# Placing the last attention pieces of a batch ahead of one or two layer-2 pieces, and copying the last two output halves with VectorE alone

## The chip, the cores and the metric

The kernel runs on one core of a Trainium2 chip. The metric is device time in microseconds (us), the median of several executions. Before the change it is 332.97 us (three runs, 332.66 to 333.33). The profiled execution has a span of 331.5 us; all times inside it are counted from its start. The granted TensorE clock was 0.998 of full speed.

## The reference

Eight batches of 576 tokens with eight heads of 64 go through causal attention in which heads 0 to 3 see only the last 32 positions (local) and heads 4 to 7 only positions with the same remainder by 32 (strided). The attention output, 4608 tokens of 512, then goes through two layers with a leaky activation between them:

```python
scores = scale * q @ k.T                      # per batch and head, scale = 1/8
attn = softmax(where(mask, scores, -1e9))     # mask: local or strided, causal
x = (attn @ v)            # -> tokens x (heads * 64) = 4608 x 512
h = x @ w_in              # 4608 x 2048
g = maximum(h, 0) + alpha * minimum(h, 0)
out = g @ w_out           # 4608 x 512, float32
```

## The kernel before, in words

**Two streams of work on one TensorE.** The layers work on nine chunks n = 0 to 8 of 512 tokens. For each chunk there are 16 pieces of layer 1 (`lin1_piece`, L534) and then 16 of layer 2 (`lin2_piece`, L563). The attention of the eight batches is cut into small pieces, held in one fixed list (`pieces`, L389 to L514). The pieces of the list are dealt out between the pieces of the layers, always in the same order; the program order of every engine is the order of this Python code, since each instruction is wrapped in `keep`.

**A layer-1 piece** multiplies a 512-token stretch of xT by one 128-column slice of w_in: four matmuls kk = 0 to 3 (L544) into a PSUM tile "hps". Slice kk of xT holds the two heads of pair kk of a batch, so the fourth matmul needs pair 3. ScalarE writes the negative part (L554), VectorE combines it into gT (L557). This last operation, `fin`, is emitted after the attention piece that follows the layer piece (list `late`, L522 to L529). **A layer-2 piece** is a quarter, called part, of an output tile mt = 0 to 3 of 128 tokens: four matmuls (L586) into "ops". With part 3 ScalarE copies the tile to SBUF (L591) and the SyncE queue sends it to memory (L592). Both layers share one pool of three PSUM buffers, tag "hps".

**The attention pieces** of a pair g of heads (four pairs a batch, the first two local, the last two strided; b = g // 4):

- T: transposes of q or k on TensorE (`transpose_piece`, L221), copies to qT by VectorE and to kT by ScalarE.
- S g.0 and S g.1 (`score_piece`, L275): score matmuls (L295), exponential by ScalarE (L319), mask by GpSimd (L329).
- P g.0 to P g.2 (`pv_piece`, L331): matmuls with v (L345), then a reciprocal (L352) and a multiplication (L354) by VectorE.
- X g (`x_piece`, L359): transposes of the result on TensorE (L362), and a copy into xT by ScalarE for strided pairs (L366), by VectorE for local ones (L370).

From batch 2 on, pairs 0 to 2 of a batch have no X piece. Their result goes through a DMA transpose on the SyncE queue (`x_dma`, L372): directly into xT for the local pairs (L378), and for pair 2 into a tile xs (L376), which ScalarE copies into xT (`x_copy`, L381 to L385). `x_copy` of pair g - 2 is emitted with piece S g.1 (L512), so for pair 10 with S12.1. Also from batch 2 on, q and k of the strided pairs are loaded with a cast by the GpSimd queue (`load_d`, L118) and turned by two DMA transposes on the SyncE queue (`transpose_d`, L124, L128). For batch 3 these are emitted with the last P piece of pair 11 (L506), and the first to read them is S14.0.

**How the pieces are dealt out.** In chunk 0 the batch-1 pieces are dealt out by an explicit rule (L700 to L704): after layer-2 piece i that many pieces of the list, and what is left after the last piece. From chunk 1 on a counter does it (L709 to L725). `left` is the number of pieces that must be out by the end of the chunk so that the next batch is complete; the counter grows by half a share with each layer-1 piece and by a whole share with each layer-2 piece:

```python
acc += left / (23.5 - 0.5 * skip) * (0.5 if i < 16 else 1.0)
cnt = int(acc); acc -= cnt
attn_n(cnt, ab)                     # cnt pieces of the list follow here
```

`left` is 27 in chunk 1 (with skip = 4: the first four layer-1 pieces get none), 21 in chunks 2 to 5, 15 in chunk 6, and zero in chunks 7 and 8. The last piece of each of these stretches is the X piece of the batch's last pair (X11, X15 ... X31). With the divisor 23.5 it comes out behind the last layer-2 piece of the chunk.

**The end.** The last output tile (chunk 8, mt = 3) is computed in two halves of 256 columns (L570 to L584). Each half is copied by ScalarE (128 columns, L581) and VectorE (128 columns, L582) into one tile "osb" and sent by one DMA (L583).

Of the kernel before, what the change touches and what calls it, by code (L numbers as in the profile page):

```python
# [31 lines left out]
def kernel(  # L32
# [10 lines left out]
    nc = tc.nc  # L43
    keep = tc.keep_in_program_order
# [401 lines left out]
    end1 = len(pieces)  # L446


    for g in range(7, npair + 2):
# [33 lines left out]
        for i, (kind, fn) in enumerate(seq):  # L483
            extra = []
            if todo and i in nslots:
                left = len([z for z in nslots if z >= i])
# [31 lines left out]
    def attn_until(b):  # L518

        return max(i for i, (g, _) in enumerate(pieces) if g == 4 * b + 3) + 1  # L520
# [3 lines left out]
    def attn_step(end):  # L524
        if pos["i"] < end:
            pieces[pos["i"]][1]()
            pos["i"] += 1
        while late:
            late.pop(0)()  # L529
# [4 lines left out]
    def lin1_piece(n, m):  # L534
        if m == 0:
            gTs[n] = gpool.tile([128, 16, 512], F16, tag="gT", name="gT")
        c0 = (512 * n) % RING
        parts = [(c0, 0, min(512, RING - c0))]
        if c0 + 512 > RING:
            parts.append((0, RING - c0, 512 - (RING - c0)))  # L540
        hps = phpool.tile([128, 512], F32, tag="hps", name="hps")
        for kk in range(4):
            for x, (src, dst, w) in enumerate(parts):
                keep(nc.tensor.matmul(  # L544
                    hps[:, dst : dst + w],
                    win16[:, kk, 128 * m : 128 * m + 128],
                    xT[:, kk, src : src + w],
                    start=(kk == 0 and x == 0),
                    stop=(kk == 3 and x == len(parts) - 1),
                    skip_group_check=True,  # L550
                ))

        neg = npool.tile([128, 512], F32, tag="neg", name="neg")
        keep(nc.scalar.activation(neg, hps, AF.Relu, scale=-1.0))  # L554

        def fin():
            keep(nc.vector.scalar_tensor_tensor(  # L557
                gTs[n][:, m, :], neg, oma[:, m : m + 1], hps, op0=ALU.mult, op1=ALU.add))
        late.append(fin)
# [3 lines left out]
    def lin2_piece(n, i):  # L563
        mt, part = i // 4, i % 4
        last = n == NCH - 1
        if part == 0:
            ops_cur["t"] = phpool.tile([128, 512], F32, tag="hps", name="ops")
        ops = ops_cur["t"]
        r0 = 512 * n + 128 * mt
        if last and mt == 3:  # L570

            if part in (1, 3):
                return
            c0 = 128 * part
            half = phpool.tile([128, 512], F32, tag="hps", name="ops3") if part else ops
            for kf in range(16):
                keep(nc.tensor.matmul(  # L577
                    half[:, 0:256], gTs[n][:, kf, 128 * mt : 128 * mt + 128],
                    wout16[:, kf, c0 : c0 + 256], start=(kf == 0), stop=(kf == 15)))
            osb = opool.tile([128, 512], F32, tag="osb", name="osb")  # L580
            keep(nc.scalar.copy(osb[:, 0:128], half[:, 0:128]))  # L581
            keep(nc.vector.tensor_copy(osb[:, 128:256], half[:, 128:256]))  # L582
            keep(nc.sync.dma_start(out[r0 : r0 + 128, c0 : c0 + 256], osb[:, 0:256]))  # L583
            return  # L584
        for kf in range(4 * part, 4 * part + 4):
            keep(nc.tensor.matmul(  # L586
                ops, gTs[n][:, kf, 128 * mt : 128 * mt + 128], wout16[:, kf, :],
                start=(kf == 0), stop=(kf == 15)))
        if part == 3:
            osb = opool.tile([128, 512], F32, tag="osb", name="osb")  # L590
            keep(nc.scalar.copy(osb, ops))  # L591
            keep(nc.sync.dma_start(out[r0 : r0 + 128, :], osb))  # L592
# [84 lines left out]
    def attn_n(n, end):  # L677
        for _ in range(n):
            attn_step(end)
        if n == 0:  # L680
            attn_step(0)
# [17 lines left out]
        attn_n(0, end1)  # L699
    for i in range(16):  # L700
        lin2_piece(0, i)
        attn_n(0 if i < 1 else 2 if i < 10 else 1, end1)
    while pos["i"] < end1:
        attn_step(end1)  # L704
    wide["on"] = False
# [3 lines left out]
    for n in range(1, NCH):  # L709
        ab = attn_until(n + 1) if n + 1 < B else len(pieces)  # L710
        left = ab - pos["i"]
        skip = 4 if n == 1 else 0
        acc = 0.0
        for i in range(32):
            if i < 16:
                lin1_piece(n, i)
            else:
                lin2_piece(n, i - 16)
            if i >= skip:
                acc += left / (23.5 - 0.5 * skip) * (0.5 if i < 16 else 1.0)  # L720
            cnt = int(acc)
            acc -= cnt
            attn_n(cnt, ab)
        while pos["i"] < ab:
            attn_step(ab)  # L725
# [30 lines left out]
```

The softmax here doesn't subtract the row's maximum and nothing guards it: scores larger than these inputs give would overflow.

## Time and profile before

| What | Value |
|---|---|
| median time, span of the profile | 332.97 us, 331.5 us |
| TensorE busy, share of the span | 319.1 us, 96% |
| VectorE, ScalarE, GpSimd busy | 183.0, 171.8, 141.2 us |
| chain that ended last, by engine | PE 89%, ACT 4%, DVE 3%, DMA 2% |
| layer-1 matmuls (L544), layer-2 matmuls (L586) | 640 and 560 |
| output DMA of a full tile, issue to landing, median | 2.3 us |
| xs transpose, issue to landing, median | 2.7 us |

PE is TensorE's matmul row and PEld its weight loads, which overlap with it. DVE is VectorE, ACT ScalarE, POOL GpSimd, SP the SyncE queue, which only issues DMAs and waits. L544 is line 544 of the kernel, and "hps<-xT,win" is what the instruction writes and reads. A row of the timeline has the start, the duration, the engine and line, the operation and its shape, and how often it is merged ("x3"); in brackets stands the idle time of the engine before it and what ended that idle time. The chain of waits is followed back from the last instruction, so its rows are what the end of the kernel hung on. The ends of matmuls are modelled in the profile, their starts are recorded.

### The profile page before, as it was taken

How to read it: one execution, taken by the hardware profiler on the slowest of the kernel's cores; microseconds unless marked ns; L12 is line 12 of the kernel's file. 1: busy time of each engine (PE TensorE's matmuls, PEld its weight loads, DVE VectorE, ACT ScalarE, POOL GpSimd, SP SyncE). 2: the span in 40 equal slices, each digit the busy share in tenths (PEclk: the TensorE clock that was granted, in tenths of full speed). 3: DMA queues.
4: the chain of work that ended last, by engine and by line, in shares of the span. 5: the costliest groups of instructions: out<-in, count | busy, mean ns of one | idle time of the engine just before them, and what ended most of it. 6: DMA issues, size and time to landing. Idle time of an engine off the chain costs nothing.

```text
span 331.5 us, 6272 instructions
## 1 busy us (share of the span) xinstructions
PE 319.1 (96%) x2493; PEld 161.6 (49%) x2493; DVE 183.0 (55%) x358; ACT 171.8 (52%) x297; POOL 141.2 (43%) x152
## 2 busy tenths in 40 slices
PE   7899999999998999999999999999999999999995
PEld 2554455554553445444458654445444444444444
DVE  5477836477544873387428832783368238605800
ACT  2644753458456645575457544764477237415611
POOL 7932495117986366736583628332611400000000
PEclk9999999999999999999999999999999999999999
DMA  7999999699599459774978397517730130011011
GB/s 221 194 205 206 248 207 154 109 211 210 105 159 179 163 69 162 122 203 55 172 114 216 37 153 125 106 17 106 139 57 18 51 96 21 1 74 52 2 63 63
DMA packets 77596, 40.32 MB, mean 122 GB/s; under 512 B 58480, under 2 KB 69248, under 8 KB 77568
## 3 DMA queue, kind: packets, MB, share of 16 engines
q0 software_dynamic: 41728, 17.38, 49.6%
q1 hardware_dynamic: 35840, 22.55, 29.9%
q8 instruction: 19, 0.31, 0.4%
q14 instruction: 9, 0.07, 0.1%
HBM read 38.01 MB, written 9.44 MB: 143 GB/s over the span
## 4 chain that ended last, share of the span: by engine, by line
PE 89%; ACT 4%; DVE 3%; DMA 2%; issue 1%; SPq 0%; ACTq 0%
PE hps L544 37%; PE ops L586 37%; PE sp L295 4%; PE pv L345 4%; PE tp L235 2%; DMA kl<-in_k_dram 2%; DVE x L354 1%; PE wps L608 1%; PE ops L577 1%; ACT xT L366 1%; ACT osb L591 1%; PE sph L311 1%; PE sp L311 1%; ACT kT L175 1%; DVE qT L177 1%
## 5 line engine op out<-in xcount | busy, mean ns | idle before, releaser
L544 PE MATMUL hps<-xT,win 128*128 128x512 f16 (+1 forms) x640 | 134.1, 358 | 3.4 <-ACT xT L366 2.8
L586 PE MATMUL ops<-wout,gT 128*128 128x512 f16 x560 | 137.0, 379 | 0.0
L557 DVE SCALAR_TENSOR_TENSOR gT<-neg,oma,hps 128x512 f16<-128x512 f32 x144 | 105.9, 744 | 51.3 <-ACT neg L554 43.6
L554 ACT ACTIVATE neg<-hps 128x512 f32<-128x512 f32 x144 | 86.0, 597 | 46.3 <-PE hps L544 45.2
L329 POOL TENSOR_TENSOR et<-et,consts 128x576 f16<-128x576 f16 (+1 forms) x48 | 61.1, 1275 | 94.3 <-ACT et L319 94.2
L544 PEld LDWEIGHTS <-win 128*128 128x128 f16 x640 | 59.6, 98 | 60.8 <-issue 7.3
L586 PEld LDWEIGHTS <-gT 128*128 128x128 f16 x560 | 48.3, 98 | 45.9
L319 ACT ACTIVATE et<-sp 72x576 f16<-72x576 f32 (+1 forms) x56 | 36.2, 646 | 30.9 <-PE sp L295 17.0
L591 ACT COPY osb<-ops 128x512 f32<-128x512 f32 x35 | 20.5, 586 | 49.9 <-PE ops L586 46.0
L352 DVE RECIPROCAL rc<-pv 72x6 f32<-72x6 f32 (+2 forms) x80 | 14.9, 186 | 55.0 <-PE pv L345 54.9
L354 DVE TENSOR_TENSOR x<-pv,rc 96x384 f16<-96x384 f32 (+2 forms) x62 | 33.0, 532 | 2.1
L345 PEld LDWEIGHTS <-et 72*128 72x128 f16 (+1 forms) x448 | 23.6, 98 | 16.8 <-DVE x L354 1.1
L295 PEld LDWEIGHTS <-kT 64*128 64x128 f16 x448 | 10.8, 95 | 26.2 <-issue 21.2
L295 PE MATMUL sp<-qT,kT 64*128 64x72 f16 (+1 forms) x392 | 17.0, 201 | 1.9 <-ACT kT L175 1.9
L608 PE MATMUL wps<-wrm 128*128 128x512 f16 x44 | 16.2, 442 | 1.2 <-DVE wrm L620 1.2
L177 DVE COPY qT<-tp 128x1024 f16<-128x1024 f16 (+1 forms) x10 | 10.1, 1010 | 11.7 <-PE tp L235 11.7
L167 POOL DMA_DIRECT2D vl<-in_v_dram x8 | 11.2, 1396 | 11.8 <-PE xp L362 10.5
L345 PE MATMUL pv<-vs,et 72*128 72x65 f16 x256 | 15.2, 194 | 0.1
L179 POOL COPY vs<-stv 72x1024 f16<-72x1024 f16 x14 | 14.4, 1034 | 0.0
L175 ACT COPY kT<-tp 128x1024 f16<-128x1024 f16 (+1 forms) x10 | 8.4, 843 | 7.4 <-PE tp L235 7.4
L383 ACT COPY xT<-xs 128x576 f16<-128x576 f16 x6 | 7.8, 1302 | 7.6 <-DMA xs<-x16s 7.6
L345 PE MATMUL pv<-vl,et 128*128 128x65 f16 x192 | 11.1, 194 | 0.0
(73 smaller groups left out, 162.9 us busy)
## 6 DMA issues: line engine op xcount, KB each, us to landing
out_dram<-osb SPq DMA_DIRECT2D x35, 256.0 KB, 2.3
ql<-in_q_dram SPq DMA_DIRECT2D x6, 512.0 KB, 5.9
kl<-in_k_dram SPq DMA_DIRECT2D x6, 512.0 KB, 6.3
stv<-in_v_dram POOLq DMA_DIRECT2D x8, 288.0 KB, 7.1
vl<-in_v_dram POOLq DMA_DIRECT2D x6, 384.0 KB, 10.6
win<-in_moe_w_in_dram POOLq DMA_DIRECT2D x4, 512.0 KB, 9.5
wout<-in_moe_w_out_dram POOLq DMA_DIRECT2D x4, 512.0 KB, 17.1
qsd<-in_q_dram POOLq DMA_DIRECT2D x6, 288.0 KB, 6.2
```

Of the source, the lines that this page charges most:

```text
L295: keep(nc.tensor.matmul(sps[y][:, w * x : w * x + w], P.kT[hf, k0 : k0 + 128], P.qT[hf, q0 : q0 + w], start=(x == 0), stop=(x == len(grp) ...
L319: keep(nc.scalar.activation(ev.rearrange("r (y c) -> r y c", y=2), sp[0:r, :, 0:n], AF.Exp, scale=SCALE))
L329: keep(nc.gpsimd.tensor_tensor(ev, ev, m, op=ALU.mult))
L345: keep(nc.tensor.matmul(pv[:, 65 * x : 65 * x + 65], et[0:r, c : c + 128], v16[0:r, 2 * P.pr + hh, t, :] if P.strided else v16[:, 6 * (2 * ...
L352: keep(nc.vector.reciprocal(rc[0:w, 0:nb], pvv[:, :, 64]))
L354: keep(nc.vector.tensor_tensor(P.x16[0:w, c0 : c0 + 64 * nb].rearrange("r (c e) -> r c e", e=64), pvv[:, :, 0:64], rc[0:w, 0:nb].unsqueeze ...
L544: keep(nc.tensor.matmul(hps[:, dst : dst + w], win16[:, kk, 128 * m : 128 * m + 128], xT[:, kk, src : src + w], start=(kk == 0 and x == 0) ...
L554: keep(nc.scalar.activation(neg, hps, AF.Relu, scale=-1.0))
L557: keep(nc.vector.scalar_tensor_tensor(gTs[n][:, m, :], neg, oma[:, m : m + 1], hps, op0=ALU.mult, op1=ALU.add))
L586: keep(nc.tensor.matmul(ops, gTs[n][:, kf, 128 * mt : 128 * mt + 128], wout16[:, kf, :], start=(kf == 0), stop=(kf == 15)))
L591: keep(nc.scalar.copy(osb, ops))
L608: keep(nc.tensor.matmul(wps, wrm[:, 0:128], wrm, start=True, stop=True))
```

## The change

Three edits. In chunk 0, two attention pieces instead of one follow layer-2 pieces 10 to 12, so that the list's stretch is through before the last layer-2 piece. From chunk 1 on the divisor is 22.5 instead of 23.5, so that the counter runs a little faster and one or two layer-2 pieces follow the last attention piece of a batch. This is meant to let the work on that last piece end under layer-2 matmuls instead of in front of the next chunk's layer 1. And the last two output halves are each copied by one VectorE copy of 256 columns, instead of 128 by ScalarE and 128 by VectorE.

```diff
@@ lin2_piece, the last output tile
             osb = opool.tile([128, 512], F32, tag="osb", name="osb")
-            keep(nc.scalar.copy(osb[:, 0:128], half[:, 0:128]))
-            keep(nc.vector.tensor_copy(osb[:, 128:256], half[:, 128:256]))
+            keep(nc.vector.tensor_copy(osb[:, 0:256], half[:, 0:256]))
             keep(nc.sync.dma_start(out[r0 : r0 + 128, c0 : c0 + 256], osb[:, 0:256]))
@@ chunk 0
     for i in range(16):
         lin2_piece(0, i)
-        attn_n(0 if i < 1 else 2 if i < 10 else 1, end1)
+        attn_n(0 if i < 1 else 2 if i < 13 else 1, end1)
@@ chunks 1 to 8
             if i >= skip:
-                acc += left / (23.5 - 0.5 * skip) * (0.5 if i < 16 else 1.0)
+                acc += left / (22.5 - 0.5 * skip) * (0.5 if i < 16 else 1.0)
```

The pieces around the places that matter, before and after (l1 m and l2 i are the pieces of layer 1 and 2, and what is named follows behind them):

| Stretch | Before | After |
|---|---|---|
| chunk 0 | l2 10 X6, l2 11 X7, l2 12 P4.0, l2 13 P4.1, l2 14 P5.0, l2 15 P5.1 X4 X5 | l2 10 X6 X7, l2 11 P4.0 P4.1, l2 12 P5.0 P5.1, l2 13 X4, l2 14 X5, l2 15 nothing |
| chunk 1 | l2 9 P10.2 S12.0, l2 10 P11.0, l2 11 S12.1 (with x_copy of pair 10), l2 12 P11.1, l2 13 P11.2 S13.0, l2 14 P12.0, l2 15 X11 | l2 8 P10.2, l2 9 S12.0 P11.0, l2 10 S12.1 (with x_copy), l2 11 P11.1, l2 12 P11.2 S13.0, l2 13 P12.0, l2 14 X11, l2 15 nothing |
| chunks 2 to 5, layer 1 (chunk 2 named) | l1 8 P13.0, l1 11 S14.1, l1 13 P13.1, l1 15 S15.0 | l1 8 P13.0, l1 10 S14.1, l1 12 P13.1, l1 14 S15.0 |
| chunks 2 to 6, end (chunk 2 named) | l2 14 P16.0, l2 15 X15 | l2 13 P16.0, l2 14 X15, l2 15 nothing |

In chunk 2, S14.0 stands behind layer-1 piece 6 before and after.

## The prediction

> **What bounds the kernel now.** I read the page first, then the chain of waits in order of time, the list of who waited for whom, and the timeline at the places where the chain leaves TensorE.
>
> ```profile
> PE 319.1 (96%) x2493; PEld 161.6 (49%) x2493; DVE 183.0 (55%) x358; ACT 171.8 (52%) x297; POOL 141.2 (43%) x152
> ```
>
> TensorE is busy 96% of the span and every other engine about half, so time can only come out of stretches in which a matmul starts later than it could. The yardstick is in the chain:
>
> ```profile
> 66.59 5.12 PE hps L544 x23
> ...
> 286.22 13.81 PE ops L586 x64
> ```
>
> 64 matmuls of 512 columns in 13.81 us are 0.216 us each, so a layer piece of four takes 0.863 us. All delays below are start to start against 0.216, since the idle time that the page gives hangs on modelled ends of matmuls. The longest repeated TensorE wait in the list of waits is the one the change aims at:
>
> ```profile
> PE hps L544 <- ACT xT L366: 2.8, 6, 1.2
> ```
>
> Six waits, one at each boundary between chunks 1 to 6 and the next. The boundary after chunk 2 in the timeline:
>
> ```profile
> 137.45 0.59 ACT L591 COPY osb<-ops 128x512 f32<-128x512 f32 x1 [1.34 <-PE ops L586]
> 137.47 0.82 PE L544 MATMUL hps<-xT,win 128*128 128x512 f16 x3
> 137.93 0.64 ACT L366 COPY xT<-xp 128x576 f16<-128x576 f16 x1
> ...
> 138.63 0.59 PE L544 MATMUL hps<-xT,win 128*128 128x512 f16 x2 [0.35 <-ACT xT L366]
> ```
>
> Three layer-1 matmuls run, the fourth (kk=3) reads the xT slice that L366 is still writing, because X15 was placed behind the last layer-2 piece and ScalarE first copies that piece's output. Loss: 138.63 - (137.47 + 3 x 0.216) = 0.51 us. After chunk 1 the same wait is longer; ScalarE and the SyncE queue there:
>
> ```profile
> 97.65 0.59 ACT L591 COPY osb<-ops 128x512 f32<-128x512 f32 x1 [1.30 <-PE ops L586]
> ...
> 101.64 1.31 ACT L383 COPY xT<-xs 128x576 f16<-128x576 f16 x1 [2.85 <-DMA xs<-x16s]
> 102.86 0.64 ACT L319 ACTIVATE et<-sp 128x576 f16<-128x576 f32 x1
> 103.40 0.57 ACT L591 COPY osb<-ops 128x512 f32<-128x512 f32 x1
> 103.87 0.65 ACT L366 COPY xT<-xp 128x576 f16<-128x576 f16 x1
> ```
>
> ```profile
> 95.99 1.24 SPq L376 DMA_TRANSPOSE xs<-x16s  x1
> 98.26 0.33 SPq L592 DMA_DIRECT2D out_dram<-osb  x1
> 98.70 2.49 SPq L128 DMA_TRANSPOSE qT<-qsd  x1
> 101.28 2.48 SPq L128 DMA_TRANSPOSE kT<-ksd  x1
> ```
>
> Here x_copy (L383) holds ScalarE until xs lands at 101.62, and everything behind it is late. Note that the output copy of mt=2 (97.65) stands ahead of x_copy, and that its output DMA (98.26) stands ahead of the two transposes of batch 3.
>
> [...] L319, L591 and L366 above follow L383 one by one. [...] the output DMA issued at 93.34 lands at 99.40, with the v load of 90.34 to 100.86 beside it.
>
> **The change, part by part.** It adds no instruction to the loops: attention pieces keep their order, only the pieces of the layers between which they stand move. I worked the new places out from the counter (rate = left / 22.5 instead of / 23.5, for chunk 1 27/20.5 = 1.32 instead of 27/21.5 = 1.26 per layer-2 piece).
>
> *Chunk 0 (13 for 10).* Before, X4 and X5 stand behind the last layer-2 piece. X5 needs VectorE's last multiplication; twelve transposes start at 64.71, and the second hps matmul starts at 66.59 where 64.71 + 12 x 0.043 + 0.216 = 65.44 was possible: 1.15 us lost. After: P4 behind piece 11, P5 behind 12, X4 behind 13, X5 behind 14. VectorE needs 4 x 0.74 us (0.19 + 0.55) from about 60.9, so is through at 63.9; X5 starts at 64.1, and its copy ends about 65.1, before layer 1 needs it (65.4). Gain 1.15.
>
> *Boundaries after chunks 2 to 6.* The X piece stands behind layer-2 piece 14, 0.863 us of matmuls earlier, and ahead of the output copy on ScalarE. L366 (0.64) then ends before piece 15 does. Gain 4 x 0.51 + 0.39 (chunk 3, whose 256-column matmuls wait 0.39) = 2.43.
>
> *Layer 1 of chunks 2 to 5.* A P piece puts 0.73 us of VectorE work ahead of the gT operation that frees an hps buffer:
>
> ```profile
> 147.94 2.16 DVE L557 SCALAR_TENSOR_TENSOR gT<-neg,oma,hps 128x512 f16<-128x512 f32 x3
> ```
>
> The first of these ends near 148.68 and the piece three further on starts at 148.72 instead of 148.53. Before, three layer-1 pieces in a row (9, 10, 11) follow that P. After, the score piece comes behind piece 10 instead of 11 and its 0.33 us fill the wait. Gain 4 x 0.2 = 0.8. In chunk 6 both such waits stay (three pieces in a row there as before).
>
> *Tail.* Before: ScalarE 0.27, then VectorE 0.29 behind it, since they write one tile:
>
> ```profile
> 327.78 0.27 ACT L581 COPY osb<-ops 128x128 f32<-128x128 f32 x1 [1.48 <-PE ops L577]
> 328.08 0.29 DVE L582 COPY osb<-ops 128x128 f32<-128x128 f32 x1 [1.46 <-ACT osb L581]
> ```
>
> 0.59 us in all. One VectorE copy of 256 columns isn't in the trace. [...] From above: 0.29 + 0.13 (128 more columns, by the slope between L354's 0.42 for 256 and 0.55 for 384) = 0.42. I take 0.42, since the measurement decides. Gain 0.17; the first half's copy lies under 1.7 us of matmuls and gains nothing.
>
> *Chunk 1, where a wait is added.* S12.1 moves from behind layer-2 piece 11 to behind piece 10, and x_copy goes with it. Piece 11 is the one that emits the mt=2 output copy, so that copy now stands BEHIND x_copy. Behind the copy on SyncE stands its output DMA, behind that the two transposes of batch 3, and for those waits S14.0 behind layer-1 piece 6 of chunk 2 (110.58 before; kT landed at 108.11). Step by step, with L the landing of xs:
> P10.2 goes one piece earlier and chunk 0 gave 1.15, so xs is issued at 94.0 instead of 95.99. But its packets share the engines with the v load, whose end moves by 1.15 only, to 99.7 (GpSimd works without a gap from the first mask of the chunk, so its issues follow that start). Before, xs landed 0.76 after the v load: L = 100.4. The lower bound is the median landing of xs in the other chunks, 94.0 + 2.7 = 96.7; the upper one 101.0.
> Then x_copy takes 1.22 to the next start, the copy 0.6, the output DMA and hand-over 0.5: transposes are issued at L + 2.3 = 102.7 instead of 98.70. From the issue of qT to the landing of kT the other chunks show 7.6 to 9.0 us, this one 9.4; I take 8.8. So kT lands at 111.5, and S14.0 starts 0.9 later than before, although TensorE without that wait would be there at about 109.4 (kk=3 waits until L + 2.96 = 103.4, and S14.0 comes 6.0 after it). The 1.15 of chunk 0 and what boundary 1 lost (0.22 at kk=2 and 1.35 at kk=3) are thus not only not regained; 0.9 is added.
>
> Sum for the likeliest case: -0.9 + 2.43 + 0.8 + 0.17 = 2.5 us gained, 332.97 - 2.5 = 330.5.
>
> **Rivals.**
> *All is gained.* xs lands early (L near 97): the output copy is only 1 us late, kT lands near 107.8 and S14.0 hardly waits. Then 1.15 + 1.57 + 2.43 + 0.8 + 0.17 = 6.1, and with some 0.4 left waiting 5.7: 327.3. For it: in every other chunk xs lands 2.7 us after its issue. Against: there it is issued when the v load is nearly done, here in its middle.
> *Little is gained.* L = 101, transposes slow at 9.4, and the layer-1 waits only move: loss of 2.1 at S14.0, 2.6 gained elsewhere: 332.5. Against: with the score piece in between, piece 11 would start at 148.53 + 0.33 = 148.86, after its buffer is free at 148.72.
> *Slower.* The transposes meet loads as in the trace's worst case: qT issued at 67.43, kT landed at 80.61, 13.2 us. kT lands at 115.9, 5.3 later than S14.0 stood before; 3.4 gained elsewhere: 334.9. For it: the stv load of the batch runs at the same time. Against: that load is small (it took 6.1), and the q and k loads stand behind the transposes in the queue.
>
> **Numbers.** Likeliest case 0.56, all gained 0.22, little 0.13, slower 0.09. The range reaches to the first rival and most of the second: 327.0 to 332.3. Faster by over 0.2% (below 332.3) takes the first two and half of the third, 0.84; same 0.07; slower 0.09.
>
> **What would show it.** No wait of layer 1 for L366 after chunks 2 to 6; layer-1 pieces 9 to 11 of chunks 2 to 5 without a gap[...]. In chunk 1, L591 directly behind L383 on ScalarE, transposes issued near 102.7, and a new TensorE wait of about 2 us at S14.0. If xs lands before 98, or S14.0 does not wait, the likeliest case is wrong and the time is nearer 327; a wait at the S pieces of chunks 3 to 5, whose kT landed 1.5 us ahead, would make it worse.

## The result and the profile after

The changed kernel takes 329.06 us (median of six runs, 328.5 to 331.09) against 332.94 us (six runs, 332.66 to 333.33). The ratio is 0.990, with a 95% interval of 0.987 to 0.993: 3.9 us faster. In the profiled execution the span is 326.6 us instead of 331.5. These 4.9 us are more than the medians differ, because the profiled run of after (328.5) is the fastest of its six and that of before (333.4) lies above its median. Two of the six runs, 330.86 and 331.09, show a mean granted clock of 0.995, the other four 0.999 or 1.000; the last section comes back to this.

The busy row of the page after, and its shares of the chain that ended last:

```profile
PE 316.8 (97%) x2493; PEld 161.8 (50%) x2493; DVE 182.8 (56%) x358; ACT 172.5 (53%) x295; POOL 141.2 (43%) x152
```

```profile
PE 92%; DVE 3%; ACT 2%; DMA 2%; issue 0%; SPq 0%; DVEq 0%; ACTq 0%
```

TensorE has the same 2493 matmuls, in a shorter span. ScalarE has two copies fewer, the tail's. Its share of the chain fell from 4% to 2%: waits for it are what went away.

The list of waits after. Columns: engine, line, what it waited for, total us, times, longest:

```profile
PE sp L295 <- ACT kT L175: 1.9, 4, 0.9
...
PE hps L544 <- ACT xT L366: 1.2, 1, 1.2
```

Of six waits of layer 1 for L366, one is left, at the boundary after chunk 1. The boundary after chunk 2 in the timeline after:

```profile
134.90 1.03 PE L585 MATMUL ops<-wout,gT 128*128 128x512 f16 x4
135.10 0.64 ACT L366 COPY xT<-xp 128x576 f16<-128x576 f16 x1 [1.56 <-PE xp L362]
...
135.76 2.75 PE L544 MATMUL hps<-xT,win 128*128 128x512 f16 x12
...
136.01 0.58 ACT L590 COPY osb<-ops 128x512 f32<-128x512 f32 x1 [0.27 <-PE ops L585]
```

L366 ends at 135.74, under the last layer-2 piece, and the output copy follows it on ScalarE instead of preceding it. Twelve layer-1 matmuls start 0.216 us apart, with no break at the fourth. In layer 1 of chunk 3, where before a piece waited for its buffer, eight matmuls now run between a P piece and a score piece, and nothing waits:

```profile
144.59 1.89 PE L544 MATMUL hps<-xT,win 128*128 128x512 f16 x8
146.41 0.30 PE L295 MATMUL sp<-qT,kT 64*128 64x72 f16 x8
```

Chunk 1 is where the prediction saw a cost. ScalarE's timeline, then the SyncE queue's, after:

```profile
100.14 1.30 ACT L383 COPY xT<-xs 128x576 f16<-128x576 f16 x1 [3.73 <-DMA xs<-x16s]
101.35 0.58 ACT L590 COPY osb<-ops 128x512 f32<-128x512 f32 x1
101.83 0.65 ACT L319 ACTIVATE et<-sp 128x576 f16<-128x576 f32 x1
102.37 0.64 ACT L366 COPY xT<-xp 128x576 f16<-128x576 f16 x1
```

```profile
93.87 1.21 SPq L376 DMA_TRANSPOSE xs<-x16s  x1
101.96 0.33 SPq L591 DMA_DIRECT2D out_dram<-osb  x1
102.39 1.36 SPq L128 DMA_TRANSPOSE qT<-qsd  x1
103.84 2.16 SPq L128 DMA_TRANSPOSE kT<-ksd  x1
```

L590 stands directly behind L383, as foreseen, and the transposes are issued at 102.39 (102.7 foreseen, 98.70 before). The last matmul of layer 1 that reads xT's slice of pair 11, and S14.0 further on, in TensorE's timeline after:

```profile
103.06 2.10 PE L544 MATMUL hps<-xT,win 128*128 128x512 f16 x9 [1.19 <-ACT xT L366]
...
108.33 0.81 PE L544 MATMUL hps<-xT,win 128*128 128x512 f16 x3
109.08 0.30 PE L295 MATMUL sp<-qT,kT 64*128 64x72 f16 x8
109.31 1.04 PE L544 MATMUL hps<-xT,win 128*128 128x512 f16 x4
```

The wait of kk=3 is still there, but S14.0 at 109.08 has no bracket: it waits for nothing. The trace gives the landing of kT as 108.42.

The tail after, VectorE's two copies and the output DMAs:

```profile
321.33 0.42 DVE L581 COPY osb<-ops 128x256 f32<-128x256 f32 x1 [10.79 <-PE ops L577]
321.78 2.08 SPq L582 DMA_DIRECT2D out_dram<-osb  x2
323.08 0.42 DVE L581 COPY osb<-ops 128x256 f32<-128x256 f32 x1 [1.32 <-PE ops L577]
```

Where the 4.9 us came from, by the excess of start-to-start times over 0.216 us per matmul of 512 columns. At a boundary kk=2 and kk=3 are the third and fourth matmul of the next layer 1: kk=2 reads the slice of xT that x_copy (L383) fills from xs, kk=3 the slice that L366 fills.

| Place | Lost before | Lost after | Gain |
|---|---|---|---|
| chunk 0, end | 1.15 | 0 | 1.15 |
| boundary after chunk 1, kk=2 and kk=3 | 0.22 + 1.35 | 0.06 + 1.35 | 0.16 |
| layer-1 buffer waits, chunks 2 to 5 | 0.20 + 0.20 + 0.18 + 0.20 | 0 | 0.78 |
| layer-1 buffer waits, chunk 6 | 2 x 0.20 | 2 x 0.20 | 0 |
| boundaries after chunks 2 to 6 | 4 x 0.51 + 0.39 | 0 | 2.43 |
| tail, from the start of L577 to the end of the last copy | 4.33 | 4.17 | 0.16 |
| start of the profile | | | 0.10 |

The sum is 4.8. All places are read from one profile of each kernel.

### The profile page after: what moved, and what is told of

Its sections match the earlier page's. It is cut to its first block, busy times and chain, and to the rows that moved or that the text cites. A ratio compares the mean times of both kernels' runs of the same rounds, so it can differ in the third digit from the quotient of the medians.

```text
span 326.6 us, 6269 instructions
## 1 busy us (share of the span) xinstructions
PE 316.8 (97%) x2493; PEld 161.8 (50%) x2493; DVE 182.8 (56%) x358; ACT 172.5 (53%) x295; POOL 141.2 (43%) x152
## 4 chain that ended last, share of the span: by engine, by line
PE 92%; DVE 3%; ACT 2%; DMA 2%; issue 0%; SPq 0%; DVEq 0%; ACTq 0%
PE hps L544 39%; PE ops L585 37%; PE sp L295 4%; PE pv L345 4%; PE tp L235 2%; DMA ql<-in_q_dram 2%; PE wps L607 1%; PE ops L577 1%; PE xp L362 1%; DVE x L354 1%; PE sph L311 1%; PE sp L311 1%; ACT kT L175 1%; DVE qT L177 1%; PE sph L295 1%; ACT qT L175 0%
## 5 line engine op out<-in xcount | busy, mean ns | idle before, releaser
L319 ACT ACTIVATE et<-sp 72x576 f16<-72x576 f32 (+1 forms) x56 | 36.2, 646 | 45.0 <-PE sp L295 36.7
L590 ACT COPY osb<-ops 128x512 f32<-128x512 f32 x35 | 20.5, 585 | 31.6 <-PE ops L585 31.2
L383 ACT COPY xT<-xs 128x576 f16<-128x576 f16 x6 | 7.8, 1300 | 7.7 <-DMA xs<-x16s 7.7
```

The lines of the kernel that those rows point to most:

```text
L319: keep(nc.scalar.activation(ev.rearrange("r (y c) -> r y c", y=2), sp[0:r, :, 0:n], AF.Exp, scale=SCALE))
```

## The experiments

### The changed kernel again

The changed kernel as it is, on the chip that also ran two of its variants below: the swapped copy and the first move of the v load. It is the base for these two.

> The changed kernel again, on the chip of the next two. Theory: 329 as before, no wait at S14.0 in chunk 2, one of about 1.35 us at the boundary after chunk 1. Rival for its two times near 331 with a clock of 0.995: they come from S14.0 waiting for a late transpose; then a profile near 331 shows that wait. Otherwise such a profile shows a stretch at a lower clock.

Measured: 328.89 us (328.5 to 329.48) against 332.99, ratio 0.987 (0.984 to 0.990). In the profile S14.0 does not wait, and the boundary after chunk 1 loses 0.33 us at kk=2 and 1.35 at kk=3. None of these six runs is near 331, so what made two of the first six longer isn't answered here. About 4 us is the gain, and the predicted 2.5 is not.

### Chunk 0 alone

```diff
-        attn_n(0 if i < 1 else 2 if i < 10 else 1, end1)
+        attn_n(0 if i < 1 else 2 if i < 13 else 1, end1)
```

> The kernel before with the chunk-0 rule alone. Theory (TensorE starts add up): the second layer-1 matmul of chunk 1 starts 1.15 us earlier, and since the end of the batch-4 v load, and with it the landing of xs, moves along, the boundary after chunk 1 keeps its waits and the 1.15 stays: about 331.8. Rival (the boundary after chunk 1 is tied to a transfer that does not move): xs lands at 101.6 as before, and the gain is lost there: 332.9.

Measured: 331.78 us (331.18 to 332.26) against 333.11, ratio 0.9960 (0.9946 to 0.9974); span 330.3 against 331.5. The waits of chunk 0 are gone and those at the boundaries are untouched, as the list of waits says:

```profile
PE hps L544 <- ACT xT L366: 2.8, 6, 1.2
```

xs landed at 100.42 instead of 101.62: it moved along with the start of the chunk, so the 1.2 us are kept through boundary 1. The prediction had them lost again at the S14.0 wait; that loss does not exist here, where x_copy still stands behind the output copy.

### The divisor alone

```diff
-                acc += left / (23.5 - 0.5 * skip) * (0.5 if i < 16 else 1.0)
+                acc += left / (22.5 - 0.5 * skip) * (0.5 if i < 16 else 1.0)
```

> The kernel before with the divisor 22.5 alone. Theory: 2.43 us from the boundaries after chunks 2 to 6, 0.8 from layer 1 of chunks 2 to 5, about 0.2 in chunk 1, no wait at S14.0, because the two transposes of batch 3 need only some 6 us when they are issued after the v load: 3.4 gained, 329.5. Rival (as I predicted): they need 8.8, S14.0 waits for 1 to 2 us, 331 to 331.5.

Measured: 331.26 us (330.5 to 332.4), ratio 0.9946 (0.9928 to 0.9964). This missed the expected 329.5. It falls where the rival had put it, 331 to 331.5, but not by the rival's cause: S14.0 did not wait here either (kT landed at 110.24). Boundaries 2 to 6 and layer 1 gained as they should; boundary 1 did not. TensorE's timeline there:

```profile
102.29 0.59 PE L544 MATMUL hps<-xT,win 128*128 128x512 f16 x2
103.60 0.38 PE L544 MATMUL hps<-xT,win 128*128 128x512 f16 x1 [0.71 <-ACT xT L383]
105.16 3.75 PE L544 MATMUL hps<-xT,win 128*128 128x512 f16 x9 [1.19 <-ACT xT L366]
```

xs was issued earlier than before (95.14, before 95.99) but landed later (102.22, before 101.62). The two matmuls lost 0.88 and 1.35 us, 2.23 together, where before lost 1.57. So 0.65 us were lost where 0.2 were expected to be gained. The last row shows a second loss: nine matmuls in 3.75 us, where the same nine take 2.10 us in the changed kernel. The stretch behind it, from the table by windows. Columns: window, length, busy time of PE, PEld, DVE, ACT and POOL with instruction counts, the granted clock, the DMA share and GB/s:

```profile
105.40:108.90 3.50, 3.50 (x13) 1.05 (x13) 1.49 (x2) 1.37 (x3) 2.51 (x3) 0.51 0.97 180
```

The same window of the changed kernel:

```profile
105.40:108.90 3.50, 3.50 (x23) 1.60 (x22) 2.90 (x6) 2.72 (x5) 1.68 (x2) 1.00 0.92 147
```

For 3.41 us, from 105.46 to 108.87, TensorE ran at half its clock (granted 0.51 in the window above, 1.00 in that of the changed kernel). By the clock that costs half of it, 1.7 us; the nine matmuls took 1.65 longer. So the profiled run adds up: 2.43 + 0.78 - 0.65 - 1.7 = 0.9, and its span is 1.0 shorter. It is the longest of the six (332.4 us). The other five, 330.5 to 331.37, are 1.7 to 2.6 us below before, where the terms without the slow stretch make 2.56; their mean clock is 1.000, they have no profile, and what some of them lack stays open.

### The layer-1 share alone

The layer-1 pieces get the larger share, the layer-2 pieces the old one, so that the X pieces stay behind the last layer-2 piece.

```diff
-                acc += left / (23.5 - 0.5 * skip) * (0.5 if i < 16 else 1.0)
+                acc += left / ((22.5 if i < 16 else 23.5) - 0.5 * skip) * (0.5 if i < 16 else 1.0)
```

> The divisor 22.5 for the layer-1 share of the counter alone, 23.5 for the layer-2 share: the score pieces of layer 1 move forward by one piece in chunks 2 to 5, the last attention piece stays behind the last layer-2 piece. Theory (a score piece fills the wait for an hps buffer): the 0.2 us waits at layer-1 piece 11 go in four chunks, 0.8 gained, 332.1, and the six waits for L366 stay at 2.8 us in the list of waits. Rival (the wait only moves to a later layer-1 piece): 0 gained.

Measured: 332.65 us (20 runs) against 333.11, ratio 0.9985 (0.9975 to 0.9995), so 0.2 to 0.8 us. In the profile the buffer waits of chunks 2 to 5 are gone, those of chunk 6 and the six boundary waits stay; the span is 330.6, 0.9 less. The waits of layer 1 were a term of their own, separate from the boundaries, of about the size taken.

### The tail alone

```diff
-            keep(nc.scalar.copy(osb[:, 0:128], half[:, 0:128]))
-            keep(nc.vector.tensor_copy(osb[:, 128:256], half[:, 128:256]))
+            keep(nc.vector.tensor_copy(osb[:, 0:256], half[:, 0:256]))
```

> The last two half tiles by one VectorE copy each, nothing else. Theory: from the last matmul's start to the end of the last copy 0.17 us less, one copy of 0.42 us for 0.59. [...] Too small for the times; read in the profile.

Measured: one run, 333.4 us, span 331.5. A single run can't show 0.17 us; the timeline can:

```profile
324.20 3.66 PE L577 MATMUL ops<-wout,gT 128*128 128x256 f16 x32
...
327.95 0.42 DVE L581 COPY osb<-ops 128x256 f32<-128x256 f32 x1 [1.32 <-PE ops L577]
```

From the start of the 32 matmuls to the end of the last copy it takes 327.95 + 0.42 - 324.20 = 4.17 us, against 328.08 + 0.29 - 324.04 = 4.33 before. The 0.16 is there; the span took it back at the boundary after chunk 1, where kk=2 lost 0.38 us for 0.22 before.

### The output copy ahead of x_copy again

In the changed kernel, x_copy of pair 10 is emitted one piece of the list later. On ScalarE this swaps two instructions and nothing else: L590 goes first.

```diff
-                    copyP = next((i for i, z in enumerate(seq) if z[0] == "S2"), 0)
+                    copyP = next((i for i, z in enumerate(seq) if z[0] == "S2"), 0) + (1 if g == 12 else 0)
```

> The changed kernel, with x_copy of pair 10 emitted one attention piece later, so that on ScalarE the output copy of mt=2 stands ahead of it again (one swap on ScalarE, nothing else moves). Theory: the output copy leaves L366's path, the wait at the boundary after chunk 1 falls by 0.55 us to 0.8; the two transposes of batch 3 are issued near 97.5 instead of 102.4, beside the v load, and need about 9.4 us again instead of 6.0, landing near 107: 0.5 gained on the changed kernel, 328.5. Rival (the swap costs nothing, L366 hangs on xs alone): no difference. If the transposes need 6 us here too, what makes them short is not the v load.

Measured: 328.68 us (328.2 to 329.55), ratio 0.986 (0.983 to 0.990), against 328.89 of the changed kernel on the same chip: not told apart. ScalarE's timeline:

```profile
96.72 0.59 ACT L590 COPY osb<-ops 128x512 f32<-128x512 f32 x1 [0.25 <-PE ops L585]
...
100.32 1.30 ACT L383 COPY xT<-xs 128x576 f16<-128x576 f16 x1 [3.02 <-DMA xs<-x16s]
101.53 0.64 ACT L319 ACTIVATE et<-sp 128x576 f16<-128x576 f32 x1
102.08 0.63 ACT L366 COPY xT<-xp 128x576 f16<-128x576 f16 x1
```

The swap brings L366 forward by 0.29 to 0.56 us (102.08, for 102.37 and 102.64 in the two profiles of the changed kernel); in this profile the loss at kk=3 falls from 1.35 to 0.86 us, near the 0.8 expected. The transposes are now issued at 97.77 instead of 102.39, 4.6 us earlier. They take 8.61 us, neither the 9.4 expected nor 6, and land at 106.38 instead of 108.42, only 2.0 earlier; S14.0 waits in neither kernel. So what the prediction made its largest cost, the output copy and with it the transposes behind x_copy, costs nothing at S14.0. It costs up to half a us at kk=3, which the times don't show.

### The v load out of the way

If xs lands late because of the load of v (384 KB by the GpSimd queue, landed at 99.19, just ahead of xs at 100.12), moving that load must bring xs forward. First to behind the transposes of batch 3:

```diff
-                    if g % 4 == 2 and c + 2 < B:
+                    if g % 4 == 2 and c + 2 < B and g != 10:
                         load_v(c + 2, False)
+                    if g == 12:
+                        load_v(4, False)
```

> The changed kernel, with the v load of batch 4 (384 KB, local heads) emitted behind the two transposes of batch 3 instead of with P9.1. Theory (xs is held up by the packets of the v load): xs lands 2.7 us after its issue, near 96.6 instead of 100.1, x_copy is through before the last layer-2 piece, the wait of 1.35 after chunk 1 goes: 1.4 gained on the changed kernel, 327.6. Rival (xs is held by the qsd and ksd loads or by the output DMA ahead of it): it lands at 99 or later and the wait stays at 1 us or more.

Measured: 333.04 us (330.15 to 335.16, 22 runs), ratio 0.9992 to before (0.9974 to 1.0011): the whole gain is gone. Half of the reason was right: xs, issued at 93.95, landed at 96.96 and the wait at boundary 1 vanished. But the v load now ran from 100.39 to 112.65, beside the two transposes, and kT landed at 111.00. In the list of waits and in TensorE's timeline:

```profile
PE sp L295 <- DMA kT<-ksd: 3.2, 1, 3.2
```

```profile
111.05 0.36 PE L295 MATMUL sp<-qT,kT 64*128 64x72 f16 x8 [3.22 <-DMA kT<-ksd]
111.34 3.48 PE L546 MATMUL hps<-xT,win 128*128 128x512 f16 x8
```

This is the S14.0 wait that the prediction feared, made by a load and not by a late issue (qT was issued at 99.24, 3.2 us earlier than in the changed kernel). And again a slow stretch follows: eight matmuls in 3.48 us, where eight took 1.89 ahead of the wait, at half clock from 111.16 to 114.58 (the mean granted clock from 111.00 to 114.60 is 0.53).

The wait, less what boundary 1 gained, is the smaller part of what was lost. Of the 22 runs, two have a mean clock of 0.999, and they take 330.15 and 330.17 us, 1.3 more than the changed kernel. Eleven have 0.993 to 0.995 (median 332.34) and nine 0.990 (median 333.81), as one and two stretches of half clock would give (an estimate: 3.41 us at 0.5 in 330 us make 0.995, two of them 0.990). So some 2.9 us of the 4.2 go with the lower clock. Why two runs escaped it isn't shown.

Second, the load still later, with piece P12.1 in layer 1 of chunk 2. There it is issued at 106.35, behind the landing of xs and 0.70 us ahead of kT's:

```diff
-                    if g == 12:
+                    if g == 13:
                         load_v(4, False)
```

> The changed kernel, with the v load of batch 4 emitted with P12.1 in layer 1 of chunk 2, behind the landing of xs and, if they need some 8 us, of the two transposes of batch 3. Theory (whichever transfer shares the engines with the v load is late, xs in the changed kernel, kT in the run before): xs lands near 97 and the boundary after chunk 1 has no wait, kT lands near 107, and S14.0 waits for 0 to 0.3 us: 1.2 to 1.4 gained on the changed kernel, 327.6, and no stretch of half clock. Rival (the loads at the start of chunk 2 hold up the transposes as much as the v load does): kT at 109 or later, S14.0 waits for over 1 us, no gain on the changed kernel.

Measured: **326.99 us** (326.77 to 327.06) against 332.92, ratio 0.982 (0.981 to 0.983); span 325.3. This beats both kernels: the interval lies below the two of the changed kernel (0.987 to 0.993, 0.984 to 0.990). The SyncE queue of this kernel, then two rows of the DMA view (what, queue, times, us from issue to landing), first of this kernel and then of the changed one:

```profile
93.97 1.21 SPq L376 DMA_TRANSPOSE xs<-x16s  x1
98.93 0.33 SPq L593 DMA_DIRECT2D out_dram<-osb  x1
99.36 1.69 SPq L128 DMA_TRANSPOSE qT<-qsd  x1
101.14 3.76 SPq L128 DMA_TRANSPOSE kT<-ksd  x1
```

```profile
xs<-x16s SPq DMA_TRANSPOSE x1, 3.1
...
kT<-ksd SPq DMA_TRANSPOSE x1, 5.9
```

```profile
xs<-x16s SPq DMA_TRANSPOSE x1, 6.3
...
kT<-ksd SPq DMA_TRANSPOSE x1, 4.6
```

xs takes 3.1 us instead of 6.3 and lands at 97.09; kT lands at 107.05; no matmul waits at boundary 1 or at S14.0. The span fell by 1.3, about the 1.4 us that boundary 1 had lost. That the v load is what holds xs up is shown: the same transpose, issued at the same time within 0.1 us, takes 3.0 and 3.1 us without it and 6.3 us with it. In the nine profiles with the v load in its old place, xs lands between 0.14 us before and 1.20 us after the end of that load, whenever xs was issued.

### Chunk 6 too

The last kernel, with a faster counter in chunk 6, where three layer-1 pieces in a row still followed a P piece:

```diff
-                acc += left / (22.5 - 0.5 * skip) * (0.5 if i < 16 else 1.0)
+                acc += left / ((15.0 if n == 6 else 22.5) - 0.5 * skip) * (0.5 if i < 16 else 1.0)
```

> As the run before, and the divisor 15 in chunk 6 alone, so that its attention pieces come behind every second layer-1 piece instead of every third. Theory of the hps wait (it arises where three layer-1 pieces follow a P piece): the two waits of 0.2 us that the changed kernel keeps in chunk 6 go, 0.4 gained on the run before, 327.2. Rival (VectorE has then more P work in layer 1 and falls behind): as many or more waits, no gain.

Measured: 327.36 us (326.73 to 329.29), ratio 0.985 (0.982 to 0.987); span 325.0. The two waits of 0.20 us are gone and the span is 0.3 shorter, but on the times it can't be told from the run before; one of its five runs is 329.29, at a clock of 0.994.

### More lead still

The changed kernel with the divisor 21.5.

```diff
-                acc += left / (22.5 - 0.5 * skip) * (0.5 if i < 16 else 1.0)
+                acc += left / (21.5 - 0.5 * skip) * (0.5 if i < 16 else 1.0)
```

> The changed kernel with the divisor 21.5, the last attention piece one more layer-2 piece ahead. Theory (one piece of lead covers the 0.65 us of L366 at the boundaries after chunks 2 to 6, and after chunk 1 the landing of xs decides, not the lead): the waits of the changed kernel, 328.9. Rival (more lead takes from the wait after chunk 1): it falls by up to 1 us, 328.

Measured: 329.64 us (328.87 to 331.49), ratio 0.991 (0.989 to 0.994), nothing over the changed kernel's 329.06. xs was issued 0.75 us earlier (93.12) and landed 1.3 later (101.42; the v load ran until 101.56), so kk=2 lost 1.13 us besides kk=3's 1.35. The profiled run, 331.39 us, has a half-clock stretch from 105.29 to 108.71 (granted 0.50). More lead in the order of pieces buys nothing while xs lands when the v load does.

## Why the prediction was right in direction and too small

**Right, within 0.02 us: the boundaries (2.43 taken, 2.43 found), the layer-1 waits (0.8, found 0.78), the tail (0.17, found 0.16), chunk 0 (1.15, found 1.15).** The isolated runs bear the separate terms out: chunk 0 alone, the layer-1 share alone, and the copy of 0.42 us in the tail.

**Right: the chain in chunk 1 up to the issue of the transposes.** xs issued at 93.87 (94.0 taken), landed at 100.12 (100.4), x_copy ahead of the output copy, transposes issued at 102.39 (102.7), kk=3 at 103.06 (103.4). The choice of a late L against the 2.7 us of the other chunks was right, and for the reason given: the moved v load shows it. This also settles the first rival: its total of 327.3 needed an early xs. The kernel with the v load at P12.1 has that early xs, and takes 326.99.

**Wrong in size: the term of 8.8 us from the issue of qT to the landing of kT.** It measured 6.03 us (102.39 to 108.42). With 8.8, kT landed at 111.5, S14.0 waited 2 us and chunk 1 gave -0.9. With 6.03, kT landed 0.66 us before TensorE got to S14.0 (109.08), the wait is zero, and S14.0 starts 1.5 us earlier than before (110.58). The difference of 2.4 us, added to the predicted 2.5, gives 4.9, the gain of the profile. The sign named for this case came true: S14.0 does not wait. "Nearer 327" did not, since kk=3 keeps its 1.35 us; the time lies between the two cases. It lies inside the stated 327.0 to 332.3 because that range was wide, and in that there is luck: what happened is none of the four cases, but the late xs of the likeliest one together with the S14.0 without a wait of the first rival.

Why 6.03? I had taken the duration as a property of the transposes, from chunks in which they are issued early, beside loads. In the twelve profiles of this batch they take 5.7 to 11.8 us, by what else is under way (times in us from the span's start):

| Kernel | qT issued | kT landed | us | v load | stv load |
|---|---|---|---|---|---|
| v load behind the transposes | 99.24 | 111.00 | 11.76 | 100.39 to 112.65 | 99.60 to 105.56 |
| layer-1 share alone | 98.62 | 109.08 | 10.46 | until 101.11 | 100.98 to 108.88 |
| before | 98.70 | 108.11 | 9.41 | until 100.86 | 101.06 to 107.17 |
| tail alone | 98.70 | 108.10 | 9.40 | until 101.06 | 101.06 to 107.10 |
| chunk 0 alone | 97.55 | 106.81 | 9.26 | until 99.69 | 99.92 to 105.63 |
| copy ahead | 97.77 | 106.38 | 8.61 | until 99.33 | 99.58 to 105.21 |
| v load with P12.1, chunk 6 too | 99.46 | 107.29 | 7.83 | from 106.42 | 99.70 to 105.01 |
| v load with P12.1 | 99.36 | 107.05 | 7.69 | from 106.35 | 99.63 to 105.24 |
| after | 102.39 | 108.42 | 6.03 | until 99.19 | 99.51 to 104.25 |
| after, again | 102.66 | 108.69 | 6.03 | until 99.28 | 99.51 to 104.31 |
| divisor alone | 104.49 | 110.24 | 5.75 | until 101.02 | 100.80 to 105.47 |
| divisor 21.5 | 103.70 | 109.41 | 5.71 | until 101.56 | 98.95 to 103.69 |

The loads do not wait for the transposes: stv goes out between 98.95 and 101.06 in all twelve, whenever the transposes do. Transposes issued later meet less of it. So a late issue is partly paid back: but for the first row, issues spread over 6.9 us (97.55 to 104.49) and landings over 3.9 (106.38 to 110.24). The swapped copy shows the same by one instruction moved: 4.6 us of issue are 2.0 us of landing. This is what my 8.8 left out: with other loads beside them, the same two transposes took from 5.71 to 11.76 us. From 88 to 112 us of before, the packets of the two busy DMA queues took 63.2% and 55.8% of the time of the 16 engines, 119% together, so packets were under way side by side. That the v load lengthens the transposes is shown by the two kernels that move it: qT issued at 99.24 and 99.36, the same stv load beside it, 11.76 us with the v load and 7.69 with only its first 0.7 us. The part of the small stv load is only read off the table; no kernel moved it alone. The same holds for the 512 KB load of ql, which stands behind kT on the SyncE queue and runs beside it for 1.9 to 6.8 us. So the v load is shown as a cause, and the step from 7.7 to 6.0 us is not taken apart.

**The second rival and the slower one** both rested on slow transposes, 9.4 and 13.2 us, and fell with them. The S14.0 wait is real, though: the kernel with the v load behind the transposes waits 3.2 us there and has no gain left.

## What to carry to other kernels

When a change delays the issue of a transfer, don't add the old transfer time to the new issue time (here 9.41 us became 6.03): ask which loads will still be under way then, and read the duration from issues that met that company. Before an instruction that waits for a transfer is moved ahead of others, list what stands behind it on its engine (here L590, L319 and L366 started at 101.35, 101.83 and 102.37, one by one behind x_copy at 100.14) and on the queues that these feed (here the transposes, at 102.39), and then check the slack of each consumer; here the delay of 3.7 us at the issue was harmless by 0.66 us. And where a small awaited transfer runs beside a long load that nobody needs yet, moving the load until the awaited transfers are all but in can add to moving the consumers: 1.3 us of span here, on top of the change, while moving it beside the next awaited transfers cost 4, most of it by the lower clock behind the wait.

## What the runs showed of the hardware

**Behind waits of 2.2 us on TensorE, a stretch at half the clock cost 1.7 us more.** In three profiles the granted clock fell to 0.5 for one stretch of 3.41 or 3.42 us while matmuls ran, and not again until the last of them: from 105.46 behind waits of 0.88 and 1.35 us (divisor alone), from 105.29 behind 1.13 and 1.35 (divisor 21.5), and from 111.16 behind one of 3.2 (v load behind the transposes). In the two cases with the divisor TensorE also ran matmuls between the waits. The 3.41 us just ahead of the slow stretch, from the divisor alone, and below it 3.41 us around the waits of the tail alone, which no slow stretch follows; the columns are those of the table by windows above:

```profile
102.05:105.46 3.41, 1.51 (x7) 0.56 (x6) 0.00 (x0) 3.22 (x5) 0.79 (x1) 1.00 0.73 141
```

```profile
102.50:105.91 3.41, 2.00 (x9) 0.77 (x8) 0.14 (x1) 2.77 (x5) 2.16 (x2) 1.00 1.27 116
```

The matmul row is busy for 1.51 us of 3.41 in the one and 2.00 in the other. Ahead of the other two slow stretches it is 1.30 (divisor 21.5) and 0.19 (v load behind the transposes). Wherever 3.41 us are laid over the profile of before or of after, from the first full clock to the last matmul, it is at least 2.16 (before, from 101.15) and 2.22 (after, from 101.00), and neither has a slow stretch. So here a slow stretch followed 1.51 us of busy time or less and none followed 2.00 or more, with the modelled ends of matmuls counted in. What between the two would bring one, and what sets its length, is not shown. The profiles with 1.0 to 1.7 us of waiting at this place (before, tail alone, after, after again, copy ahead) have none.

A stretch of 3.41 us at half the clock in 327 us makes a mean clock of 0.995. The two runs of the changed kernel near 331 us have just this mean, and are about 2 us longer than the others. So they probably had such a stretch; no profile of the changed kernel caught one, and this is not shown. Wherever 3.41 us are laid over this place in the two profiles of the changed kernel, the matmul row is busy for at least 2.05, more than ahead of any of the three slow stretches. By these three, such a run would have had to wait longer at this place, which is an estimate. The kernel with the v load at P12.1, which has no wait at either place, had no such run among its four, and its times lie within 0.3 us. But one run of the kernel with chunk 6 changed as well had a clock of 0.994, though its profile, of another run, shows neither wait; so this boundary need not be the only place.
